# Turning the row maxima of an attention kernel with one 128x32 transpose and sixteen small moves on SyncE's queue

## The chip, the cores and the metric

The kernel runs on one core of a Trainium2 chip. The metric is the device time of one execution in microseconds; lower is better. The core has five engines with an instruction queue each: TensorE (PE in the profile, with its weight loads as PEld), VectorE (DVE), ScalarE (ACT), GpSimd (POOL) and SyncE (SP), which here only issues DMA transfers. POOL issues some transfers too, on a queue of its own.

## The reference

```python
def _A_ref(x, wqkv, wo):                  # x is the layernormed input, [1, 2048, 512]
    qkv = (x @ wqkv).reshape(B, S, 3, H, Dh).transpose(2, 0, 3, 1, 4)   # H = 32, Dh = 16
    q, k, v = qkv[0], qkv[1], qkv[2]
    scores = jnp.einsum("bhqd,bhkd->bhqk", q, k) * Dh ** -0.5
    p = softmax(scores, axis=-1)
    o = jnp.einsum("bhqk,bhkd->bhqd", p, v)
    return o.transpose(0, 2, 1, 3).reshape(B, S, D) @ wo

def _B_ref(x, w1, b1, w2, b2):
    h = layernorm(x)
    u = gelu(jnp.einsum("bsd,sf->bdf", h, w1) + b1)       # F = 1792
    y = jnp.einsum("bdf,fs->bds", u, w2) + b2
    return y.transpose(0, 2, 1)

xn = layernorm(x)
return x + _A_ref(xn, wqkv, wo) * silu(_B_ref(xn, w1, b1, w2, b2))
```

Everything is float32. It is a full softmax attention of 32 heads, gated by a token-mixing MLP.

## The kernel before, in words

Float32 values are split into an upper and a lower part of 32-bit words that TensorE multiplies in one pass (fp32r), so a precise product is three products of parts. For q and k the three are stacked along the contraction: a head has 16 numbers, and 48 rows hold upper and lower parts of them. Two heads form a pair; head a = 0 lives on rows 0 to 63 and a = 1 on rows 64 to 127 of the tiles `qs[p]` and `ks[p]` (128 x 2048, named `big` in the trace), p = 0 to 15.

Softmax needs the maximum of each query's scores first. So each pair is gone through twice:

- *Maxima.* `max_of` (L537 on PE, L541 on DVE) multiplies a block of 128 queries with 512 keys over 48 rows and reduces the result to one maximum per query, in `mxp`. After eight blocks (a *span* of 1024 queries; two spans a pair, 32 in all) `max_rows` turns the maxima into rows. L555 reduces the four parts to `neg` (128 queries x 16: two heads x eight blocks, negated; the tile has 32 columns). A transpose on DVE (L552) writes `f`; POOL makes the upper part (cast, L562) and the lower part (subtraction, in `sub`, L107) in `m`; moves (`move`, L111) write them into rows 64a + 48 (upper, t = 0) and 64a + 49 (lower, t = 1) of `qs[p]`, 1024 columns each. The same rows of `ks[p]` hold ones.
- *Scores.* `score` multiplies 128 keys with 512 queries over 50 rows (L1000), so the product comes out with the maximum already subtracted; ACT takes the exponential (L1005), and `values` multiplies by v (L1015) into the bank `av`. `put_away` stores a span's result and denominators on SyncE's queue; later `divide` loads them again (tiles `u`, `sq`, `uo`) and POOL divides.

The scores follow the maxima by LEAD = 22 steps, where a step is a block of 128 queries and half the keys. The first steps of the main loop therefore have maxima alone (the lead), the middle has both, with matmuls of the MLP mixed in as a written-out string of letters says, and the last ones have scores alone, with output products (L1215, L1389) in strings of their own (`ENDING`).

In the middle, a piece of `max_rows` is taken from the list `pieces` at given places, one at a time, where also `values` and postponed work (`run_later`) are called. The first piece is called where the list is filled, at the end of every eighth round of the loop; in the lead and after the last maxima the list is emptied at once:

```python
        if s < NU and s % 16 == 14:
            pieces.extend(max_rows(s + 1))
            piece()
        while t < 0 and piece():
            pass
```

The order of work on each engine is the order of the program; a framework adds the waits. It gives the transfers of SyncE and ACT eight completion counters in turn, and those of POOL eight others. At the end, the loop calls `load_second` and four times `load_out` (each of these four issues two loads of 128 x 512 on SyncE's queue, L952 and L954) before the pieces of the last span. In `part`, POOL multiplies a partial output by its gate and adds x (L922, L923); it reads the tiles `gt` and `xt` that two of these loads fill again.

## Time and profile before

| | |
|---|---|
| median of 3 runs | 1633.11 us (1633.03 to 1633.38) |
| the profiled execution | 1634.06 us, of which the span of the trace is 1632.2 us |
| granted TensorE clock | 0.998 |
| PE busy | 1621.9 us (99%) |
| DVE busy | 1418.1 us (87%) |
| ACT busy | 1194.5 us (73%) |
| POOL busy | 575.4 us (35%) |
| transposes L552 | 128 of 32x32, 25.3 us in all |
| moves L111 of `m` | 128 on POOL's queue, 66.2 us in all |

Busy time counts work, not waits; issuing a transfer is not counted. A row of a group gives line, engine, operation, output and inputs, shape, count, then total us and mean ns, then idle time before it with its cause. A row of a timeline gives start, duration, engine, line, operation and count; the bracket behind it is idle time before it and who ended it. PEld and PEldq are TensorE's weight loads and their waits.

### The profile page before, as it was taken

Reading aid. Unit: us, or ns where it says so; the run is one execution under the profiler, and the core shown is the slowest. Engines: PE = TensorE matmul, PEld = TensorE weight load, DVE = VectorE, ACT = ScalarE, POOL = GpSimd, SP = SyncE. Lnnn points to the kernel's source line nnn. Section 1 sums busy time; section 2 is a strip of 40 time slices with the busy share of each in tenths; the row PEclk is TensorE's granted clock in tenths of the full one; section 3 lists DMA queues with packets and bytes.
Section 4 is the critical chain, followed back from the end, with each engine's and each line's share of the span. In section 5 each row is a group of like instructions: output and inputs, shape, how many; then the busy total and the mean of one; then the engine's idle time right before and its main releaser. Section 6 shows DMA issues by size and latency. Waiting matters only on the chain.

```text
span 1632.2 us, 31813 instructions
## 1 busy us (share of the span) xinstructions
PE 1621.9 (99%) x11948; PEld 892.0 (55%) x11948; DVE 1418.1 (87%) x2506; ACT 1194.5 (73%) x2297; POOL 575.4 (35%) x676
## 2 busy tenths in 40 slices
PE   9999999999999999999999999999999999999998
PEld 7888845555554545555555545555554545544554
DVE  7655989999999999999999999999999999999955
ACT  4333488777877777787777777787777777788785
POOL 0223743333443334332433223223222332662434
PEclk9999999999999999999999999999999999999999
DMA  6479621415133141836150522305152515354344
GB/s 226 174 247 227 122 59 47 82 34 95 41 53 76 38 79 35 191 121 111 37 85 18 99 57 46 70 30 77 37 85 59 91 37 78 100 110 134 117 151 168
DMA packets 150775, 152.89 MB, mean 94 GB/s; under 512 B 51340, under 2 KB 109708, under 8 KB 147548
## 3 DMA queue, kind: packets, MB, share of 16 engines
q1 hardware_dynamic: 146044, 149.70, 38.8%
q8 instruction: 94, 1.54, 0.4%
q0 software_dynamic: 4288, 0.62, 0.3%
q14 instruction: 61, 0.50, 0.1%
q10 hardware_dynamic: 288, 0.52, 0.1%
HBM read 99.63 MB, written 50.32 MB: 92 GB/s over the span
## 4 chain that ended last, share of the span: by engine, by line
PE 98%; DVE 1%; ACT 0%; DMA 0%; SPq 0%; issue 0%; DVEq 0%; ACTq 0%
PE av L1015 31%; PE sc L1165 16%; PE sc L1000 10%; PE sc L537 8%; PE mx L1000 8%; PE mx L1165 7%; PE mx L537 6%; PE sc L440 3%; PE mx L440 2%; PE mx L1112 1%; PE sc L1112 1%; PE sc L1215 1%; PE av L440 1%; PE sc L116 1%; PE sc L114 1%; PE sc L115 1%
## 5 line engine op out<-in xcount | busy, mean ns | idle before, releaser
L541 DVE TENSOR_REDUCE mxp<-sc 128x1 f32<-128x512 f32 x1129 | 735.9, 681 | 74.7 <-PE sc L537 49.7
L1005 ACT ACTIVATE prob<-sc 128x512 f32<-128x512 f32 x1135 | 638.3, 604 | 168.8 <-PE sc L1000 98.2
L541 DVE TENSOR_REDUCE mxp<-mx 128x1 f32<-128x512 f32 x919 | 606.0, 681 | 50.3 <-PE mx L537 30.9
L1005 ACT ACTIVATE prob<-mx 128x512 f32<-128x512 f32 x913 | 523.1, 606 | 127.3 <-PE mx L1000 71.7
L1015 PE MATMUL av<-prob,vp 128*32 128x512 f32 x4096 | 543.0, 604 | 0.0
L537 PE MATMUL sc<-big 48*128 48x512 f32 x1129 | 427.8, 417 | 0.0
L1000 PE MATMUL sc<-big 50*128 50x512 f32 x1135 | 423.1, 417 | 0.2 <-ACT prob L1005 0.2
L1165 PE MATMUL sc<-hu,wh 64*128 64x512 f32 x1072 | 359.3, 404 | 0.0
L537 PE MATMUL mx<-big 48*128 48x512 f32 x919 | 349.9, 416 | 0.1
L1000 PE MATMUL mx<-big 50*128 50x512 f32 x913 | 346.9, 415 | 0.5 <-ACT prob L1005 0.5
L1000 PEld LDWEIGHTS sc<-big 50*128 50x128 f32 x1135 | 198.2, 185 | 137.9 <-DVE mxp L541 102.0
L537 PEld LDWEIGHTS sc<-big 48*128 48x128 f32 x1129 | 196.9, 185 | 81.7 <-ACT prob L1005 53.5
L1165 PEld LDWEIGHTS sc<-hu,wh 64*128 64x128 f32 x1072 | 193.9, 184 | 58.8 <-issue 41.9
L1000 PEld LDWEIGHTS mx<-big 50*128 50x128 f32 x913 | 162.2, 185 | 107.4 <-DVE mxp L541 83.3
L1165 PE MATMUL sc<-hu,wl 64*128 64x512 f32 x536 | 215.1, 401 | 0.0
L537 PEld LDWEIGHTS mx<-big 48*128 48x128 f32 x919 | 160.9, 185 | 74.4 <-ACT prob L1005 38.1
L1015 PEld LDWEIGHTS av<-prob,vp 128*32 128x32 f32 x4096 | 81.8, 108 | 171.8 <-issue 161.4
L1165 PE MATMUL mx<-hu,wh 64*128 64x512 f32 x464 | 156.2, 405 | 0.0
L179 POOL CAST wh<-raw 128x512 fp32r<-128x512 f32 (+1 forms) x105 | 61.3, 584 | 255.2 <-PE sc L537 57.7
L107 POOL TENSOR_TENSOR wl<-raw,wh 128x512 fp32r<-128x512 f32 (+1 forms) x113 | 136.6, 1210 | 28.9 <-ACT wh L181 20.4
L562 POOL CAST m<-f 16x128 fp32r<-16x128 f32 x32 | 9.0, 280 | 311.2 <-DVE f L552 308.4
L1165 PEld LDWEIGHTS sc<-hu,wl 64*128 64x128 f32 x536 | 98.8, 184 | 13.3 <-issue 5.9
(240 smaller groups left out, 1592.0 us busy)
## 6 DMA issues: line engine op xcount, KB each, us to landing
raw<-in_B_w_dram SPq DMA_DIRECT2D x93, 256.0 KB
big<-k_d SPq DMA_DIRECT2D x96, 128.0 KB
big<-q_d SPq DMA_DIRECT2D x96, 128.0 KB
q_d<-sg SPq DMA_DIRECT2D x16, 512.0 KB
k_d<-sg SPq DMA_DIRECT2D x16, 512.0 KB
num_d<-ev SPq DMA_DIRECT2D x30, 256.0 KB
u_d<-uo SPq DMA_DIRECT2D x14, 512.0 KB
hu<-u_d SPq DMA_DIRECT2D x14, 512.0 KB
```

Source lines behind the costliest of these rows:

```text
L107: eng.tensor_tensor(out=o, in0=a, in1=b.bitcast(F32), op=OP.subtract)
L114: nc.tensor.matmul(ps, wh, mh, start=first, stop=False)
L115: nc.tensor.matmul(ps, wh, ml, start=False, stop=False)
L179: nc.gpsimd.tensor_copy(whs[n][:, :m, :], raws[n][:, :m, :])
L440: nc.tensor.matmul(ps, w[part][:, kd, m], xt[kd][:, z, :], start=w is wh and z == 0 and kd == 0, stop=w is wl and kd == ND - 1,)
L537: nc.tensor.matmul(ps, q[o : o + 48, r * P : (r + 1) * P], k[o : o + 48, c * 512 : (c + 1) * 512], start=True, stop=True,)
L541: return nc.vector.tensor_reduce(mxp[u // 16][:, a, r % 8, c : c + 1], ps, axis=AX.X, op=OP.max)
L1000: nc.tensor.matmul(ps, ks[p][o : o + 50, kb * P : (kb + 1) * P], qs[p][o : o + 50, at : at + 512], start=True, stop=True,)
L1005: return nc.scalar.activation(e, ps, AF.Exp, scale=scale)
L1015: nc.tensor.matmul(av[32 * j : 32 * j + 32, :], vps[p][:, kbs[c], 16 * a : 16 * a + 32], prob.pop((t, a, c)), start=first, stop=last,)
L1112: nc.tensor.matmul(ps(a), w(r), m(r), start=first, stop=last)
L1165: i = nc.tensor.matmul(ps(), w(r), m(r), start=first and first_half, stop=last and not first_half)
```

## The change

`f` becomes 128 x 32 and is written by one transpose of the whole of `neg`. That transpose works on 32x32 blocks in place: partition 32g + i of `f` holds column i of the queries 32g to 32g + 31 of each block, for i = 8a + block. So a row of 1024 maxima lies in four groups of eight partitions, 32 queries in each, and the moves become sixteen (head a, part t, group g) of 8 partitions x 32 values, in place of four of 8 partitions x 128. They are issued on SyncE's queue and not on POOL's. POOL's cast and subtraction now work on 128 partitions x 32 in place of 16 x 128. The pieces become two where there were five, so the one transpose stands in the place of the first of the four, and POOL's part and the moves, which stood with the fourth, come three places earlier.

```diff
-        f = sm.tile([32, P], F32, name="f", bufs=1)
-        def turned(c):
-            nc.vector.transpose(f[:, 32 * c : 32 * c + 32], neg[32 * c : 32 * c + 32, :])
+        f = sm.tile([P, 32], F32, name="f", bufs=1)
...
         def last():
-            turned(3)
-            m = sm.tile([16, 2, P], F32R, name="m", bufs=1)
-            nc.gpsimd.tensor_copy(m[:, 0, :], f[:16, :])
-            sub(nc.gpsimd, m[:, 1, :], f[:16, :], m[:, 0, :])
+            nc.vector.transpose(f, neg)
+            m = sm.tile([P, 2, 32], F32R, name="m", bufs=1)
+            nc.gpsimd.tensor_copy(m[:, 0, :], f)
+            sub(nc.gpsimd, m[:, 1, :], f, m[:, 0, :])
             for a in range(2):
                 for t in range(2):
                     row = 64 * a + 48 + t
-                    move(
-                        qs[p][row : row + 1, span * 1024 : (span + 1) * 1024],
-                        m[8 * a : 8 * a + 8, t, :], nc.gpsimd,
-                    )
-        return first_, *(lambda c=c: turned(c) for c in range(3)), last
+                    to = qs[p][row : row + 1, span * 1024 : (span + 1) * 1024]
+                    to = to.rearrange("o (r g b) -> o r g b", r=8, g=4)
+                    for g in range(4):
+                        at = 32 * g + 8 * a
+                        move(to[:, :, g, :], m[at : at + 8, t, :], nc.sync)
+        return first_, last
```

## The prediction

> **What bounds the kernel now.** I read the page first: busy times, then the chain that ended last, then a window of the steady part.

> ```profile
> span 1632.2 us, 31813 instructions
> PE 1621.9 (99%) x11948; PEld 892.0 (55%) x11948; DVE 1418.1 (87%) x2506; ACT 1194.5 (73%) x2297; POOL 575.4 (35%) x676
> PE 98%; DVE 1%; ACT 0%; DMA 0%; SPq 0%; issue 0%; DVEq 0%; ACTq 0%
> 300.00:1400.00 1100.00, 1100.00 (x8412) 559.17 (x8412) 1003.61 (x1712) 861.15 (x1653) 356.94 (x442) 1.00 0.35 70
> ```

> The last row gives, for 300 to 1400 us, the length and then the busy time of PE, PEld, DVE, ACT and POOL, the granted clock (1.00), the DMA share and GB/s. PE is busy for all 1100.00 us at full clock, and the chain is 98% PE. DVE is busy 1003.61 us of them, which leaves it 9% idle. So an instruction taken off DVE or POOL is worth nothing here unless PE waits for it, and a wait put in front of PE costs its full length.

> Next I followed one span (1024 queries of a head pair, one of 32) from its transposes to its scores, in the timelines of DVE, POOL and PE's load queue.

> ```profile
> 812.87 0.19 DVE L552 STREAM_TRANSPOSE f<-neg 32x32 f32<-32x32 f32 x1
> 820.76 0.28 POOL L562 CAST m<-f 16x128 fp32r<-16x128 f32 x1 [12.99 <-DVE f L552]
> 821.12 0.45 POOL L107 TENSOR_TENSOR m<-f,m 16x128 fp32r<-16x128 f32 x1
> 821.52 2.07 POOL L111 DMA_DIRECT2D big<-m  x4
> DMA to landing us min/median/max: 1.6/1.6/1.6
> L1000 PEldq EVENT_SEMAPHORE  x2: 51/51/51, 826.0 to 827.7; - x2
> ```

> Columns are start and duration in us; the last two rows are the landing of these four moves and PE's waits for the row data, one for each head. First transpose 812.87 (call it T0); the cast at 820.76 had waited 12.99 us for the fourth; the last of four moves issued by 823.59 and landed about 1.6 after its issue, near 824.7. PE asks at 826.0, T0 + 13.1. The margin in this span is about 1.3 us.

> **The change, part by part.**

> *Transposes.* Three of four go, 32 times, at the mean of this row; the one left covers 128 partitions, but still 32 values in each, so I take the 0.19 of one 32x32.

> ```profile
> L552 DVE STREAM_TRANSPOSE f<-neg 32x32 f32<-32x32 f32 x128 | 25.3, 198 | 3.0
> PEld sc L1000 <- DVE mxp L541: 102.0, 125, 0.8
> PEld mx L1000 <- DVE mxp L541: 83.3, 100, 0.8
> ```

> DVE gets 96 x 0.198 = 19.0 us back. The two rows of waits (total us, times, longest) show PE's weight loads waiting for DVE to free a bank, never over 0.8 us; PE's matmuls cover it, since PE is busy for 1100.00 of 1100. Between nothing and −19 I take −0.2 for the steady part, nearest the row of full PE. If one 128x32 cost four times as much (0.8) DVE would save nothing, and this term becomes 0.

> The transpose that is left stands where the first of four stood, so f is ready at T0 + 0.2 and not at T0 + 7.9 (820.76). Cast and subtraction on POOL are of 32 columns where they were of 128: 0.28 and 0.45 are their upper bounds, a third of that the lower; POOL was idle 12.99 us before them. The first move can go at T0 + 0.6 to T0 + 0.9.

> *The lead.* Before scores begin, PE follows DVE:

> ```profile
> 150.00:190.00 40.00, 40.00 (x350) 36.91 (x346) 39.71 (x69) 14.57 (x25) 21.16 (x19) 1.00 0.92 209
> 184.36 3.69 DVE mxp L541 x6
> 188.33 0.84 DVE L552 STREAM_TRANSPOSE f<-neg 32x32 f32<-32x32 f32 x4
> ```

> DVE is busy 39.71 of 40 us and the chain runs over its reductions from 184.36. Four transposes took 0.84; one takes 0.2: −0.6 us, once.

> *POOL's four issues.* 128 issues of about 0.52 go (2.07 for four). POOL is busy 357 of 1100 us, so this buys nothing by itself.

> *Sixteen moves on SyncE's queue.* SyncE issues in order, each DMA holding it for a time, and the kernel's framework hands its DMAs eight completion counters in turn: a DMA waits until the one eight before it has landed (first row: 33 such waits of SyncE, 22.2 us in all). No row shows a move of 8 partitions of 128 bytes on this queue; bounds from its other rows:

> ```profile
> SPq L111 <- DMA big<-q_d: 22.2, 33, 1.7
> 807.80 0.37 SPq L170 DMA_DIRECT2D raw<-in_B_w_dram  x1
> 831.87 1.09 SPq L730 DMA_DIRECT2D d<-ev  x2
> 836.71 0.42 SPq L111 DMA_DIRECT2D big<-q_d  x1
> 837.18 0.42 SPq L111 DMA_DIRECT2D big<-k_d  x1
> 900.07 0.63 SPq L780 DMA_DIRECT2D sq<-num_d  x1
> 900.75 0.58 SPq L784 DMA_DIRECT2D uo<-rec_d  x1
> ```

> Start to start: 0.47 (16-row loads), 0.57 (the small two of d<-ev, 1.09 for two), 0.68 (sq<-num_d). I take 0.57, the pitch of the smallest transfer; the range is 0.47 to 0.68. Landing 1.6 as POOL's moves. The last of sixteen lands at T0 + 0.6 + 15 x 0.57 + 1.6 = T0 + 10.8 (9.3 by 0.47, 12.4 by 0.68): before T0 + 13.1, in every span where the queue is free. SyncE issued nothing between the rows at 807.80 and 831.87, so this span is free: cost 0. Were POOL still at a weight's subtraction when f comes, the first move would go about 1 us later, also inside the margin. The cover ends at a pitch of (13.1 − 2.2) / 15 = 0.73.

> [...]

> *Spans where the queue isn't free.* At 902.03 a division's loads stand ahead:

> ```profile
> 902.03 0.19 DVE L552 STREAM_TRANSPOSE f<-neg 32x32 f32<-32x32 f32 x1
> 908.00:910.00 2.00, 2.00 (x18) 0.96 (x18) 1.97 (x5) 1.44 (x4) 0.08 (x1) 1.00 0.55 162
> 910.00:912.00 2.00, 2.00 (x20) 1.32 (x20) 2.00 (x4) 1.96 (x5) 1.92 (x5) 1.00 0.18 53
> L1000 PEldq EVENT_SEMAPHORE  x2: 51/51/51, 915.2 to 916.9; - x2
> ```

> The load of uo issued at 900.75 and the weight load right after it are the last ahead; DMA runs at 162 GB/s until 910 and falls to 53 after it, so I put their landing at 910 to 910.6. They hold the counters of moves 7 and 8. Moves 9 to 16 follow, the last at 910.6 + 8 x 0.57 = 915.2, landed 916.8. PE asks at 915.2, and the first row it asks for can be that of the moves that come last (the lead of the two heads alternates). Late by 0.8 to 1.6: +1.4. The same stands at 1257.83, behind

> ```profile
> 1256.55 0.58 SPq L784 DMA_DIRECT2D uo<-rec_d  x1
> 677.10 5.89 SPq L111 DMA_DIRECT2D hu<-u_d  x3
> L1000 PEldq EVENT_SEMAPHORE  x2: 51/51/51, 693.3 to 694.4; - x2
> ```

> which is +1.0. At 679.3 the queue is held till 683.0 by loads of hu that wait for their buffer: the last move at 683.1 + 15 x 0.57 = 691.7, landed 693.3 to 695.0 beside those loads, against 693.3: +0 to 1.7, I take +0.8. One more such span near 1391: +0.3. SyncE's later loads and stores go up to 10 us later; they are issued one mixer step or more ahead, so I take 0 for them.

> *The end.* The last span has its transposes in one piece, and its sixteen moves stand in program order behind nine loads of 256 KB.

> ```profile
> 1566.86 0.84 DVE L552 STREAM_TRANSPOSE f<-neg 32x32 f32<-32x32 f32 x4
> 1570.33 0.32 SPq L954 DMA_DIRECT2D sq<-y_d  x1
> 1576.01 0.32 SPq L952 DMA_DIRECT2D xt<-g_d  x1
> 1571.27 2.04 POOL L111 DMA_DIRECT2D big<-m  x4 [2.63 <-PE sc L1215]
> 1569.00:1571.00 2.00, 2.00 (x22) 0.99 (x15) 1.23 (x5) 1.16 (x4) 0.00 (x0) 1.00 1.00 307
> DMA to landing us min/median/max: 3.3/3.8/4.3
> 1578.80 0.50 PE L1000 MATMUL mx<-big 50*128 50x512 f32 x1
> 1579.20:1583.60 4.40, 4.40 (x38) 2.08 (x35) 0.73 (x3) 4.24 (x9) 1.74 (x2) 1.00 0.51 165
> ```

> SyncE stopped between 1570.33 and 1576.01 for POOL (L923), which must have read xt before a new load goes into it. L922 and L923 stood on POOL behind the four moves, from 1571.27 + 2.04 = 1573.31 to 1576.0, 2.7 us for both. Without the moves POOL can be through with them as early as 1566.86 + 0.9 + 2.7 = 1570.5 if their data is there, so I let the last two loads go near 1571, the moves behind them; were POOL no sooner than before, the loads would land after 1578 and the term grow by 1 to 2. Nine loads x 128 x 512 x 4 bytes = 2.36 MB at 307 GB/s are 7.7 us from about 1567.4, plus some 2 until landing: about 1577.2 for the last. Move 8 waits for that one's counter; moves 9 to 16 follow it: 1577.2 + 8 x 0.57 + 1.6 = 1583.4 for the last (1582.6 at 0.47, 1584.2 at 0.68). PE needs the rows at 1578.80: late by 4.6 (3.8 to 5.4). In the old order POOL's moves, beside the same loads, took 3.3 to 4.3 and came in time. After it PE is busy 4.40 of 4.40 us a pair of steps: nothing gives it back. I take +4.3, a little less, since PE's queue holds values to run.

> **Sum.** −0.2 − 0.6 + 1.4 + 1.0 + 0.8 + 0.3 + 4.3 = +7.0. The profiled execution took 1634.06 us (span 1632.2), 0.95 above the median 1633.11; the difference is applied to the median: 1633.11 + 7.0, or about 1640.

> **The rivals.**

> *No difference (within 0.2%, 3.3 us, about what a measurement of this kernel can tell).* Pitch 0.47, the division's loads land by 909, and the eight loads of the end land by 1573 so that moves 9 to 16 land near 1578.8: each late term becomes 0 to 1, leaving −0.8 to +3.3: 1632.3 to 1636.4. For: the moves' bytes are few. Against: the 307 GB/s row.

> *Faster.* DVE really gates PE: the 185 us of weight loads waiting for its reductions are on the path, and each transpose taken out lets the next matmul begin sooner. At full 19.0 minus the end's 4: about 1618; it decides if over 11 us of 19 come through. For: the rows of L1000 waits. Against: PE without a gap over 1100 us.

> *Much slower.* Four moves each write 32-value pieces of one and the same row; if the framework takes pieces that interleave for overlapping, three of each four wait for the one before to land: 12 x (0.57 + 1.6) + 4 x 0.57 + 1.6 = 30, some 17 us after PE asks, 30 x 17 = +510: 2140 us. Against it, from the start of the kernel, timelines of ACT and POOL:

> ```profile
> 51.04 0.58 ACT L342 COPY v<-mx 128x512 f32<-128x512 f32 x1
> 53.16 0.33 POOL L341 MEMSET v<- 128x256 f32 x1
> ```

> The two write interleaving pieces of 16 of one tile, the memset first in the program, and the copy went 2.1 us ahead of it. A milder form is a pitch over 0.73: at 0.85 the last lands at T0 + 15, 1.8 late: 30 x 1.8 = +54, 1690 us.

> **How the numbers follow.** Forecast (the end and the crowded spans late, over +3.3) 0.69; no difference 0.2; faster 0.06; much slower 0.05. So slower 0.74, same 0.2, faster 0.06. The likeliest's own range is 1636.5 to 1646 (0.47 to 0.68 for the pitch, each crowded span 0 to 2 us, the end 3 to 6). It is opened below to 1632.5 for nearly all of the no-difference case and above to 1650 for a pitch a little over 0.73, which leaves out under 0.2.

> **What would show it.** L552 x32, 128x32, near 0.2 us: the transpose term. Sixteen moves in SyncE's timeline at 0.57 start to start, landing 1.6: the pitch. Idle time of PE just before scores of L1000 with moves into big as releaser, longest at the end (about 4), then in the spans of 902 and 1258: the late terms. PE busy at the same sum, the span longer by the gaps. The prediction is wrong if a 128x32 costs 0.8, if the pitch passes 0.73, if the end's loads land before 1575, or if PE's busy time itself shrinks.

## The result and the profile after

The changed kernel takes 1658.21 us (median of 4 runs, 1655.70 to 1660.27) against 1633.24 before: 25.0 us more, a ratio of 1.0151 (95% interval 1.0133 to 1.0169). The forecast was 1640, with a range up to 1650: it had the direction, but +7.0 us where 25.0 came.

The page of the changed kernel, its first rows and the chain by engine:

```profile
span 1656.3 us, 32190 instructions
PE 1632.0 (99%) x11948; PEld 891.0 (54%) x11948; DVE 1408.1 (85%) x2410; ACT 1194.7 (72%) x2297; POOL 503.2 (30%) x548
PE 88%; SPq 3%; DMA 3%; DVE 2%; POOL 2%; issue 1%; ACT 1%; DVEq 0%; POOLq 0%; ACTq 0%
```

The span grew by 24.1 us, in two parts. PE's busy time grew by 10.1 (1632.0 against 1621.9) for the same 11948 matmuls, and the time in which PE did nothing by 14.0 (1656.3 − 1632.0 = 24.3 against 10.3). The first part was in no step of the prediction, which had PE busy at the same sum.

*Where PE stood still.* The groups of L997 (the scores; L1000 before), then the timeline of PE at each stall, with the idle time before it in brackets:

```profile
L997 PE MATMUL sc<-big 50*128 50x512 f32 x1135 | 425.3, 420 | 4.2 <-DMA big<-m 4.1 <-ACT prob L1002 0.2
L997 PE MATMUL mx<-big 50*128 50x512 f32 x913 | 347.5, 416 | 9.9 <-DMA big<-m 9.6 <-ACT prob L1002 0.2
698.32 0.46 PE L997 MATMUL mx<-big 50*128 50x512 f32 x1 [1.91 <-DMA big<-m]
924.36 0.59 PE L997 MATMUL mx<-big 50*128 50x512 f32 x1 [1.89 <-DMA big<-m]
1282.57 0.46 PE L997 MATMUL sc<-big 50*128 50x512 f32 x1 [0.72 <-DMA big<-m]
1463.92 0.76 PE L997 MATMUL sc<-big 50*128 50x512 f32 x1 [3.35 <-DMA big<-m]
1600.71 0.76 PE L997 MATMUL mx<-big 50*128 50x512 f32 x1 [5.82 <-DMA big<-m]
```

Five spans of 32 have their rows late, 13.7 us together, and what ends each wait is the landing of the moves of `m`. In the other 27 the moves are hidden.

*Why they were late.* SyncE's timeline in a free span and in three of the five; duration is that of the whole train of sixteen:

```profile
819.57 10.99 SPq L111 DMA_DIRECT2D big<-m  x16
685.95 11.00 SPq L111 DMA_DIRECT2D big<-m  x16
908.54 14.44 SPq L111 DMA_DIRECT2D big<-m  x16
1587.78 11.65 SPq L111 DMA_DIRECT2D big<-m  x16
```

The pitch is 10.99 / 16 = 0.68 us. A free span bears that. At 908.54 counters held by a division's loads stretch the train by 3.4, of which SyncE waits 2.8 for `uo<-rec_d` (the span of 1282.57 is of the same kind); at 685.95 and 1587.78 it starts late, behind other loads. The fourth late span has another cause; timelines of DVE and POOL:

```profile
1445.85 0.20 DVE L556 STREAM_TRANSPOSE f<-neg 128x32 f32<-128x32 f32 x1
1446.60 1.28 POOL L107 TENSOR_TENSOR hu<-sq,hu 128x512 fp32r<-128x512 f32 x1
1449.42 1.28 POOL L704 TENSOR_TENSOR t<-t,ev 128x512 f32<-128x512 f32 x1
1450.65 0.20 POOL L558 CAST m<-f 128x32 fp32r<-128x32 f32 x1
1461.78 1.68 DMA big<-m
```

`f` is ready at 1446.05 and POOL, in order, comes to it at 1450.65: 4.6 us of work for a division and a gate stand ahead. The last row is from the chain of waits: the sixteenth move, landed at 1463.46.

*Where PE was slow.* The granted clock is the third number from the end (length first, then busy us of PE, PEld, DVE, ACT, POOL, each with its instructions). Windows of 3.41 us around three of the stalls:

```profile
695.86:699.27 3.41, 1.50 (x13) 1.05 (x10) 1.33 (x3) 1.29 (x3) 0.00 (x0) 1.00 0.45 146
699.27:702.69 3.42, 3.42 (x16) 1.02 (x15) 1.42 (x3) 1.14 (x4) 0.00 (x0) 0.50 0.93 257
1279.55:1282.96 3.41, 2.69 (x25) 1.64 (x19) 2.88 (x5) 2.21 (x5) 1.83 (x2) 1.00 0.21 70
1282.96:1286.37 3.41, 3.41 (x31) 1.35 (x27) 2.20 (x4) 2.46 (x5) 0.05 (x1) 1.00 0.32 90
1596.98:1600.39 3.41, 0.00 (x0) 0.00 (x0) 0.00 (x0) 0.00 (x0) 0.00 (x0) 0.50 0.02 2
1600.39:1603.80 3.41, 3.09 (x13) 2.32 (x13) 0.06 (x1) 2.29 (x5) 0.00 (x0) 0.50 0.55 159
1603.80:1607.22 3.42, 3.42 (x17) 0.59 (x16) 0.06 (x1) 1.73 (x4) 0.00 (x0) 0.50 0.64 201
```

After the stall of 1.91 us PE has work for all of the next 3.42 us and does 16 matmuls in it, at half clock, where 31 go at full clock (the row of 1282.96). The stall of 0.72 us leaves the clock at 1.00. After the stalls of 1.89 and 3.35 us too there is one stretch at half clock, after that of 5.82 three. Together 20.5 us at half clock, in which PE is busy for 16.7: that loses 8.4 of the 10.1 us. The other 1.7 I did not trace.

### The profile page after: what moved, and what is told of

The parts are those of the page before. It is cut to its first block, busy times and chain, and to the rows that moved or that the text cites. A ratio compares the mean times of both kernels' runs of the same rounds, so it can differ in the third digit from the quotient of the medians.

```text
span 1656.3 us, 32190 instructions
## 1 busy us (share of the span) xinstructions
PE 1632.0 (99%) x11948; PEld 891.0 (54%) x11948; DVE 1408.1 (85%) x2410; ACT 1194.7 (72%) x2297; POOL 503.2 (30%) x548
## 4 chain that ended last, share of the span: by engine, by line
PE 88%; SPq 3%; DMA 3%; DVE 2%; POOL 2%; issue 1%; ACT 1%; DVEq 0%; POOLq 0%; ACTq 0%
PE av L1012 28%; PE sc L1162 15%; PE sc L997 9%; PE sc L537 7%; PE mx L997 7%; PE mx L1162 6%; PE mx L537 6%; SPq L111 3%; PE sc L440 2%; PE mx L440 2%; PE sc L1109 1%; DMA raw<-in_B_w_dram 1%; DMA y_d<-t 1%; PE mx L1109 1%; POOL hu L107 1%
## 5 line engine op out<-in xcount | busy, mean ns | idle before, releaser
L541 DVE TENSOR_REDUCE mxp<-sc 128x1 f32<-128x512 f32 x1129 | 739.3, 684 | 91.0 <-PE sc L537 60.0
L541 DVE TENSOR_REDUCE mxp<-mx 128x1 f32<-128x512 f32 x919 | 608.4, 684 | 62.2 <-PE mx L537 40.6
L997 PE MATMUL sc<-big 50*128 50x512 f32 x1135 | 425.3, 420 | 4.2 <-DMA big<-m 4.1
L997 PE MATMUL mx<-big 50*128 50x512 f32 x913 | 347.5, 416 | 9.9 <-DMA big<-m 9.6
L997 PEld LDWEIGHTS sc<-big 50*128 50x128 f32 x1135 | 199.4, 186 | 144.5 <-DVE mxp L541 101.0
L997 PEld LDWEIGHTS mx<-big 50*128 50x128 f32 x913 | 162.7, 186 | 118.5 <-DVE mxp L541 83.2
L107 POOL TENSOR_TENSOR wl<-raw,wh 128x512 fp32r<-128x512 f32 (+1 forms) x113 | 137.0, 1213 | 40.6 <-ACT wh L181 28.2
L1162 PEld LDWEIGHTS mx<-hu,wh 64*128 64x128 f32 x464 | 84.0, 185 | 26.7 <-issue 20.1
```

The source lines that it names most:

```text
L107: eng.tensor_tensor(out=o, in0=a, in1=b.bitcast(F32), op=OP.subtract)
L541: return nc.vector.tensor_reduce(mxp[u // 16][:, a, r % 8, c : c + 1], ps, axis=AX.X, op=OP.max)
L997: nc.tensor.matmul(ps, ks[p][o : o + 50, kb * P : (kb + 1) * P], qs[p][o : o + 50, at : at + 512], start=True, stop=True,)
L1162: i = nc.tensor.matmul(ps(), w(r), m(r), start=first and first_half, stop=last and not first_half)
```

## The experiments

Theory A: the loss is the stalls of five spans and the half clock behind the long ones, and the stalls come from sixteen moves at 0.68 on a queue that has other work ahead. Theory B: the early place or the many small transfers cost by themselves. Theory C: the stalls cost their own length alone. Theory D came with the fourth run. A ratio is to the kernel before, and the two numbers behind it are its 95% interval.

**Sixteen moves on POOL's queue.**

```diff
-                        move(to[:, :, g, :], m[at : at + 8, t, :], nc.sync)
+                        move(to[:, :, g, :], m[at : at + 8, t, :], nc.gpsimd)
```

> The changed kernel with its sixteen moves issued on POOL's queue in place of SyncE's; the one early transpose stays. Theory A: the 25 us are PE's waits for rows in five spans (14.1 us) and the half-clock stretches behind the long ones (10.2 us), and the waits come from the order and the pitch of SyncE's queue. POOL's issues took 0.52 each, so the last move lands at T0 + 0.6 + 15 x 0.52 + 1.6 = T0 + 10.0, before PE asks at T0 + 13; only the span near 1446, where POOL itself is 4.6 us behind, and the last one may be late by 1 to 2 us. So 1633 to 1638. Theory B (the early place or the small transfers themselves cost, whatever the queue): 1650 or more, with the same five gaps.

Measured 1637.60 us against 1633.47 (ratio 1.0024, 1.0014 to 1.0034). POOL's timeline in the lead, PE's just after, two rows of the chain there, and POOL's issues in all:

```profile
189.52 8.03 POOL L111 DMA_DIRECT2D big<-m  x16
198.89 0.50 PE L1109 MATMUL mx<-hu,wl 64*128 64x512 f32 x2 [1.66 <-POOL wl L107]
201.04 2.00 PE mx L1109 x10
205.58 1.19 PE mx L1109 x10
L111 POOL DMA_DIRECT2D big<-m x512 | 256.6, 510 | 16.6 <-DMA big<-m 12.6 <-issue 3.8
```

The five gaps are gone but for 0.39 us at the end; 21 of the 25 us come back, so the small transfers and the early place aren't what costs (against B). What is left is of another kind: in the lead the eight microseconds of issues stand before POOL's split of a weight, PE waits 1.66 us for it, and its matmuls are slow for a while behind the wait: ten of L1109 take 2.00 us from 201.04, where ten take 1.19 from 205.58.

**The last span's pieces ahead of the nine loads.**

```diff
+        while s >= NU and piece():
+            pass
         if s >= NU - SPP + LEAD and unkept:
             load_second()
```

> The changed kernel with the last span's transpose and moves put ahead of the nine loads of the end in program order, nothing else. Theory A: the gap of 5.8 us before the last span's scores shrinks to under 1.5 us and its 10.2 us of half clock disappear, so 5 + 5 = about 10 us of the 25 come back: 1648. The other four gaps stay as they are. Theory C (the gap at the end costs its own length alone, the lower clock has another cause): 5 us come back, 1653. If the loads, now some 11 us later, are the next thing PE waits for, nothing comes back.

Measured 1648.60 us (1642.51 to 1650.63), 9.6 less than the changed kernel. The waits of its profile (total, times, longest):

```profile
PE sc L997 <- DMA big<-m: 4.0, 2, 3.3
PE mx L997 <- DMA big<-m: 3.7, 3, 1.6
201.84:205.25 3.41, 2.40 (x15) 1.18 (x13) 1.32 (x3) 2.26 (x5) 1.82 (x2) 1.00 0.95 311
205.25:212.07 6.82, 6.82 (x32) 5.64 (x30) 4.86 (x8) 5.71 (x12) 6.57 (x7) 0.50 0.63 142
```

The end's gap is 0.55 us where it was 5.82, and the granted clock over the span is 0.994 where it was 0.992; the longest wait left, 3.3 us, is that of the span near 1446, and the other three gaps stay (1.56, 1.64 and 0.70). A gap of 5.3 us taken away gave 9.6. That speaks against theory C; as four runs of each kernel spread widely, the stalls of chosen length below are the firmer test. The two windows are of this profile alone: 1.01 us of idle time in the lead had 6.82 us at half clock behind it, where the changed kernel's 0.89 there had none. That makes 3.4 us from one execution to another, and is my reading, not a test, of why these two kernels' times spread over 4.6 and 8.1 us.

**Eight moves in place of sixteen.**

```diff
-            for a in range(2):
-                for t in range(2):
...
+            for t in range(2):
+                to = qs[p].rearrange("(a x) c -> a x c", a=2)[:, 48 + t, span * 1024 : (span + 1) * 1024]
+                to = to.rearrange("a (r g b) -> a r g b", r=8, g=4)
+                for g in range(4):
+                    at = 32 * g
+                    move(to[:, :, g, :], m[at : at + 16, t, :], nc.sync)
```

> The changed kernel with eight moves in place of sixteen: each takes 16 partitions (both heads) of one part and group, to two rows 64 apart; SyncE's queue and the early place stay. Theory A: pitch 0.52 to 0.68, so the last move lands by T0 + 0.7 + 7 x 0.68 + 1.7 = T0 + 7.2 in a free span, no move waits for a counter held by a division's loads for long, and all five gaps go, also the one near 1446 (T0 + 4.9 + 4.8 + 1.7 = T0 + 11.4) and nearly all of the end's: 1632 to 1636. Theory B (SyncE's queue behind other transfers is too late whatever the number): gaps of 1 to 5 us stay in the spans with loads ahead and at the end, 1642 or more.

Measured 1632.32 us (ratio 0.9992, 0.9983 to 1.0002). SyncE's timeline and the only wait for the rows that is left:

```profile
812.57 4.45 SPq L111 DMA_DIRECT2D big<-m  x8
PE mx L995 <- DMA big<-m: 0.4, 1, 0.4
```

The whole loss is gone with place and queue as in the changed kernel: half as many moves at a pitch of 4.45 / 8 = 0.56 are in time even behind a division's loads.

**The early place alone, in the kernel before.**

```diff
         def last():
-            turned(3)
+            for c in range(4):
+                turned(c)
...
-        return first_, *(lambda c=c: turned(c) for c in range(3)), last
+        return first_, last
```

> The kernel before with its four transposes done in one piece at the place of the first, and so POOL's part and its four moves 8 us earlier; shapes and queue as before. It has the early place alone. Theory A: nothing waits for the rows, so 1632 to 1635; four transposes in a row (0.84 us) hold DVE a little longer, which PE's buffered matmul covers. Theory B with the early place as the cause: 1640 or more.

Measured 1640.72 us (ratio 1.0045, 1.0030 to 1.0060): 7.2 more, with no gap on PE beyond those of the kernel before. By its number this is the case of theory B; but the kernel with eight moves has the early place too and loses nothing. One thing that it does not have is four transposes in a row, and the next two runs look at that.

**One transpose, written four times in a row** (in the kernel with eight moves):

```diff
-            nc.vector.transpose(f, neg)
+            for _ in range(4):
+                nc.vector.transpose(f, neg)
```

> The kernel with eight merged moves, its one 128x32 transpose written four times in a row (the same result; three are idle work on DVE). The kernel before with four transposes in a row at the early place was 7.2 us slower than before, with no gap on PE. Theory D (a burst of 0.8 us on DVE delays the reductions that free PE's banks, and PE's matmuls run late without a gap in the record): 32 x 0.22 = 7 us again, 1639 to 1640. Rival (POOL's earlier work and moves cost, in that kernel, not the burst): 1632 to 1633, as with one.

Measured 1643.76 us (ratio 1.0060, 1.0045 to 1.0075), 11.4 more than with one and 4 more than expected.

**Three idle transposes, one at each later place:**

```diff
+        f2 = sm.tile([P, 32], F32, name="f2", bufs=1)
...
-        return first_, last
+        return first_, last, *(lambda: nc.vector.transpose(f2, neg),) * 3
```

> Eight merged moves as before, and three idle 128x32 transposes of the same maxima into a tile that nobody reads, one at each of the next three places of the loop: the work on DVE that the change took away, put back in its old places. Theory D (only the burst costs; a single 0.2 us beside DVE's reductions is covered): 1632 to 1633, as with one transpose. Rival (each 0.2 us on DVE is paid, and the merged version's gain over the kernel before is a part of it): 32 x 3 x 0.2 = 19 us at most, 1640 to 1651.

Measured 1632.70 us (ratio 0.9998, 0.9989 to 1.0008), 0.4 more than without them, which the spread of the runs covers. The window from 300 to 1400 us in three kernels (early place; four in a row; three spaced), the bursts in DVE's timelines of the first two, the idle transposes of the last, and PE's weight loads waiting for DVE's reductions in the whole of the second, then of the third:

```profile
300.00:1400.00 1100.00, 1099.80 (x8370) 554.38 (x8368) 999.21 (x1704) 857.44 (x1644) 352.45 (x438) 1.00 0.35 69
300.00:1400.00 1100.00, 1099.64 (x8354) 552.41 (x8347) 997.96 (x1698) 856.63 (x1642) 296.36 (x338) 1.00 0.35 69
300.00:1400.00 1100.00, 1100.00 (x8418) 558.63 (x8420) 1000.80 (x1714) 861.80 (x1655) 304.59 (x349) 1.00 0.35 69
815.68 0.83 DVE L552 STREAM_TRANSPOSE f<-neg 32x32 f32<-32x32 f32 x4
817.61 0.94 DVE L557 STREAM_TRANSPOSE f<-neg 128x32 f32<-128x32 f32 x4
L568 DVE STREAM_TRANSPOSE f<-neg 128x32 f32<-128x32 f32 x96 | 19.2, 200 | 0.1
PEld sc L996 <- DVE mxp L541: 108.9, 153, 0.8
PEld mx L996 <- DVE mxp L541: 88.9, 122, 0.8
PEld sc L996 <- DVE mxp L541: 101.2, 124, 0.8
PEld mx L996 <- DVE mxp L541: 83.2, 100, 0.8
```

Nearly the same DVE work (19.2 us) costs 0.4 us when it is spaced and 11.4 when it comes in bursts of 0.9 us. PE reads as busy in all three, but does 8354 matmuls in 1100 us with the burst and 8418 without: 0.8% fewer. And with the burst its weight loads wait 275 times for DVE's reductions, 197.8 us in all, where they wait 224 times, 184.4 us, without. So theory D holds: a burst on DVE holds up the reductions that free PE's banks, and a PE that reads as busy without a gap can still be held up. A single transpose of 0.2 us between reductions is covered: 96 of them cost 0.4 us. Why this burst costs 4 us more than that of the kernel before stays open.

**SyncE's queue alone, in the kernel before.**

```diff
-                        m[8 * a : 8 * a + 8, t, :], nc.gpsimd,
+                        m[8 * a : 8 * a + 8, t, :], nc.sync,
```

> The kernel before with its four moves (8 partitions x 128 values, late place, four transposes) issued on SyncE's queue in place of POOL's: the queue alone. At the pitch of 0.68 that the changed kernel showed the four take 2.7 us in place of 2.1, so in a free span the last lands at T0 + 8.7 + 3 x 0.68 + 1.7 = T0 + 12.4, against T0 + 13.1: in time, barely. Theory A (the queue costs where other transfers stand ahead): small gaps of 0 to 1 us in a few spans and 1 to 3 at the end, behind the nine loads: 1634 to 1640. Rival (the queue costs in every span, by SyncE's waits or the longer issue): 30 x 0.5 = 15, 1648.

Measured 1634.28 us (ratio 1.0004, 0.9995 to 1.0013): no difference that can be told. One gap more, 1.1 us near the end, is a wait for DVE and not for the rows; the small gaps expected in a few spans did not come. Four moves on SyncE cost nothing that can be told even at the late place; it is sixteen on that queue that do.

**Stalls of chosen length, in the kernel before.**

```diff
             sub(nc.gpsimd, m[:, 1, :], f[:16, :], m[:, 0, :])
+            for _ in range({8: 7, 10: 11, 13: 14, 15: 18, 18: 22, 20: 29}.get(u // 16, 0)):
+                nc.gpsimd.tensor_copy(m[:, 0, :], f[:16, :])
```

> The kernel before, with POOL repeating its cast into the upper half of m (0.28 us each, the same values) ahead of the moves in six of the 32 spans: 7, 11, 14, 18, 22 and 29 times, so the rows come 2, 3, 4, 5, 6 and 8 us later there and, past a margin of 1.3 to 2.5 us, PE stands still for about 0, 1, 2, 3, 4 and 6 us. Nothing of the change is in it. It asks what a stall does to the clock. Theory A (as in the changed kernel, where stalls of 1.89, 1.91, 3.35 and 5.82 us had half clock behind them and 0.72 and 0.98 had none): stalls of more than half of a 3.41 us stretch are followed by 3.4 us or more at half clock, so four or so of the six, and the kernel loses the stalls plus 1.7 us for each such stretch: 16 + 7 to 10, 1656 to 1660. Rival: only a stall as long as a whole stretch (3.4 us) does it: two stretches at most, and stalls of 2 to 3 us none.

Measured 1671.52 us in one run, 12 to 16 more than expected. PE's waits for the rows, and windows behind the stalls of 1.78, 2.67 and 6.01 us:

```profile
PE sc L1002 <- DMA big<-m: 16.4, 4, 7.9
PE mx L1002 <- DMA big<-m: 6.0, 1, 6.0
649.51:652.92 3.41, 1.63 (x14) 0.87 (x15) 1.69 (x4) 1.04 (x3) 3.25 (x6) 1.00 0.03 4
652.92:656.33 3.41, 3.41 (x18) 1.03 (x17) 1.55 (x3) 1.00 (x3) 1.19 (x1) 0.50 0.00 0
789.45:796.28 6.83, 6.64 (x27) 2.81 (x31) 2.90 (x5) 3.17 (x6) 6.59 (x8) 0.50 0.00 0
1024.97:1035.21 10.24, 6.42 (x27) 2.81 (x31) 2.67 (x5) 2.95 (x6) 5.79 (x8) 0.50 0.01 2
```

Five stalls came about (1.78, 2.67, 4.04, 6.01, 7.87: 22.4 us), and behind each of the three shown there is half clock, also behind the two that are shorter than 3.4 us, so the rival falls, and so does theory C. The stretches shown are 3.41, 6.83 and 10.24 us long: those behind the two longer stalls are two and three times the first, which the expectation put at one each. The granted clock over the span is 0.988, which makes about 40 us at half clock in all (2 x 0.012 x 1669.7). The span grew by 37.5, of it 14.7 in busy time. Nothing of the change is in this kernel, so the half clock belongs to the stall.

**The one transpose and sixteen moves at the late place.**

```diff
-        return first_, last
+        return first_, *(lambda: None,) * 3, last
```

> The changed kernel with its one transpose, POOL's part and the sixteen moves at the place of the old fourth transpose, three places later. It takes away the 7.7 us of cover. The last move lands at T0 + 7.7 + 0.7 + 15 x 0.68 + 1.7 = T0 + 20.3, against T0 + 13: PE stands for about 6 us (a little less, for what it has queued) in some 30 spans, and theory A puts 10.2 us at half clock behind each, of which some 2 fall into the stall itself: 30 x (6 + 4) = +300, 1930 us. Rival (the place doesn't matter, SyncE works off the moves while PE does other things): 1658, as the changed kernel.

Measured 1905.94 us in one run. PE's waits and its page row:

```profile
PE sc L997 <- DMA big<-m: 93.8, 16, 6.6
PE mx L997 <- DMA big<-m: 84.1, 14, 6.9
PE 1709.5 (90%) x11948; PEld 916.9 (48%) x11948; DVE 1410.6 (74%) x2410; ACT 1202.0 (63%) x2297; POOL 501.3 (26%) x548
```

Thirty waits of 5.9 us, 177.9 in all, and 87.6 us more of busy time. The early place is what hides sixteen moves in 27 spans. The granted clock was 0.928; the added busy time is 2.9 us a stall here, where I had put 4 for the half clock.

**Eight moves, and the last span's pieces first** (both edits shown above).

> Eight merged moves, and at the end the last span's pieces ahead of the nine loads in program order: the candidate for the best version. The 0.44 us gap that eight merged moves leave before the last span's scores goes: 1632.3 - 0.4 = 1631.9, against 1633.2 of the kernel before, a difference of 0.08% that five rounds may just show. If the loads, 4 us later, are waited for, 1633 or more.

Measured 1631.97 us against 1633.46 (ratio 0.9991, 0.9982 to 0.9999). Its median is the lowest of all, 1.5 us under the kernel before; the interval only just leaves out 1.

## Why the prediction was right and where it was wrong

- *Direction and mechanism.* In part right: the forecast had rows late in the crowded spans and at the end, longest at the end, with PE's gaps and the moves as what ends them. But the sum gave +7.0, and the trace grew by 24.1. Of the 17.1 us between them 10.1 are busy time and 5.9 are late terms sized too small; the last 1.1 is not traced.
- *The clock.* The step that failed is the rule at the start that a wait in front of PE costs its full length. It costs more: 10.1 of the 24.1 us are busy time, 8.4 of them by the half clock, for which the sum had no term. The stalls made at will show it (22.4 us of stalls, 37.5 us of span), and the gap at the end taken away agrees (5.3 us of gap, 9.6 us of time).
- *The late terms.* Forecast 0.8, 1.4, 1.0, 0.3 and 4.3, in all 7.8; measured 1.91, 1.89, 0.72, 0 and 5.82, and 3.35 in a span that the forecast did not have: 13.7. The span near 1446 failed at the sentence that POOL could be "about 1 us" late; it was 4.6.
- *The pitch.* Taken as 0.57, from the smallest transfer; it was 0.68, the upper end. The cover, up to 0.73, held, which is why 27 spans show nothing. The traces show which row was the nearest: in that of the changed kernel the counter of a move of the sixteen rises 9 times for one transfer (in all 512 of them), as that of `sq<-num_d` does in 6 of its 8, whose 0.68 was the forecast's upper end; that of `d<-ev`, whose 0.57 it took, rises 3 times. That the number of rises sets the pitch is not shown. The merged moves, of two rows each, went 0.56 apart.
- *The end.* It was put down to the counters of the loads. The train there took 11.65 us in place of 10.99, so counters held it little; it began 5.2 us after `f` was ready, behind the loads, and then took its own pitch.
- *DVE.* The transpose of 128x32 took 0.203 us as one of 32x32, and the term of −0.2 holds: three spaced transposes put back cost 0.4 us. No run separates the −0.6 of the lead. But its reason, that PE reads as busy for 1100.00 of 1100, proves less than it claimed: in the burst kernels PE reads so too and is slowed.
- *The rivals.* "Much slower" by interleaving pieces did not come: the moves went 0.68 apart, with no wait for each other. "No difference" needed a pitch of 0.47; its time is that of eight moves. "Faster" falls with the three spaced transposes: 19.2 us of DVE's work are worth 0.4.

## What to carry to other kernels

Price a stall of the bound engine with its clock: here a wait of 1.91 us on TensorE cost about 3.6, by my estimate from it and half of the 3.42 us at half clock behind it. Before moving transfers to a queue, count them, and check the crowded places (what stands ahead on that queue, and on the engine that prepares the data), not the free ones; halving their number was worth more here than a free queue (1632.32 us against 1637.60). Compare instruction counts in equal windows where an engine reads as fully busy: that is where the delay of the bursts showed (8354 against 8418 in 1100 us).
